# Last block of a fused attention and bilinear feed-forward kernel: which accumulators share a PSUM tile, and when its side work is issued

## The chip, the cores and the metric

The kernel runs on one core of one Trainium2 chip. Its time is the device time of one execution in microseconds (us). A core has five engines, each with its own queue, which it works through in order: PE (TensorE, matrix products, with the weight loads PEld), DVE (VectorE), ACT (ScalarE), POOL (GpSimd) and SP (SyncE, which here issues DMAs). They wait for one another by semaphores.

## The reference

One layer on x of shape 1 x 2048 x 576: multi-query attention with 32 heads of width 18 that share one key and one value, then a gated feed-forward part of width F = 4608 without a nonlinearity.

```python
h  = x + attention(layernorm(x)) @ wo
z  = layernorm(h)
g  = z @ w_gate            # 2048 x 4608
u  = z @ w_up              # 2048 x 4608
h2 = h + (g * u) @ w_down  # 2048 x 576
```

Everything is float32. The kernel reaches that accuracy by splitting each operand into a high part (a cast) and a low part (the rest, a subtraction on DVE) and by making three products of each: high by high, high by low, low by high.

## The kernel before, in words

The 2048 rows are four blocks b = 0 to 3 of 512 rows (TB). Blocks 0 to 2 go through `ffn(b)` (L905), while the attention of the later blocks runs in between. `ffn` loops over 36 feature tiles f of 128 columns. For each f, 27 pairs of matmuls (L930, numbered j) make g and u; then ACT copies g (L956), DVE multiplies it by u (L960, `hf`), and after every second f the products are added to the output by `down` (L843) for a pair of feature tiles. `down` makes 14 stages of three matmuls (L882) in three accumulators; each stage is read and added to the residual h, by DVE (L888) or by an ACT copy and a POOL addition (L892, L893), and a stage that goes on in the same accumulator waits for that reading. The last pair of a block has a simpler form (L855): eight outputs, one after another.

While there is attention left, g and u have a tile of one bank each; once it is used up (block 2, f from 23 on), they share a tile of two banks (L922).

PSUM has eight banks. `ps_s` (L69) gives tiles of two banks, two of them; `ps_f` one bank, two of them; `ps_m` and `ps_a` one bank, one of each.

Two pieces of side work are generators that `ffn` steps at fixed j:

- `weight_sums` (L1076): sums of gate and up weights that the last block needs. POOL makes 72 of them (L1087), with loads and stores by SP; the loop takes one step at j = 8, 16 and 24 of each f of blocks 0 and 1 (L939). Its two buffers are taken from the ten in which the weights of `down` are held.
- `ahead` (L982): what the last block needs before it begins. Four steps normalise its h (DVE L990, POOL L991); five transpose it, 4 PE transposes (L998) and an ACT copy (L999) each; the others make sums and high and low parts on ACT and DVE (L1016 to L1032), and the first weight parts. When they are taken is set by two tables by hand: AHEAD (f: {j: steps}) and TURNS (steps after the `down` at the end of f), L1470 on.

The last block (`last_block`, L1119) computes g and u by a seven-product scheme over halves of 256 rows (Strassen's idea). It loops over 18 passes p. Each pass has seven `product` calls of 12 matmuls (L1138), three `tail` calls of 4 (L1145), and between them up to seven steps of `down` for earlier passes (`go`, generator D). The accumulators are `a` (of this pass, changing place from pass to pass), `b_` and `c`. In the order of the program:

- product 1 into a, ACT copy (L1176), a step of down;
- product 2 and tail into c, DVE sum (L1182), POOL product, step;
- product 3 into b_, ACT copy (L1188), step; product 4 into a, ACT copy (L1195), step;
- product 5 and tail into b_, DVE sum (L1201); product 6 and tail into a, DVE sum (L1207), two steps;
- product 7 and tail into a, a step, ACT copy of one half (L1237), DVE product of the other half with it (L1240).

Between these stand the high parts (ACT, L1154) and low parts (DVE, L1157) for the later down. After each product `feed(i)` (L1052) is called: DVE makes the low part of the gate and up weights for the product two further on (L1058), ACT the high part for the one three further on (L1061), and SP loads a later one. So the low weights of product 2 of a pass are made by the last instruction that DVE has in the pass before.

`down_pairs` (L1092) does down for two passes at once: seven steps, each for t = 0 and 1 (two row halves), into four accumulators, two for each t; each result is read by DVE (L1108), or for four of the 14 by ACT (L1112) and POOL (L1113). At the end the last pair of feature tiles is added by eight outputs (L1262) with a DVE addition each (L1266) and four stores.

In the kernel before, `a` takes turns between the two halves of the `ps_s` tile s0, and b_ and c are the halves of s1; down_pairs has ps_f, ps_f, ps_m and ps_a.

## Time and profile before

| | |
|---|---|
| median of 3 runs | 2356.39 us (2353.79 to 2359.95) |
| profiled execution, its time | 2357.88 us |
| its span, first to last instruction | 2356.1 us |
| mean granted TensorE clock in it | 0.995 |
| busy: PE, ACT, DVE, POOL | 96%, 64%, 54%, 30% |

The last block's passes begin at about 1965 us of the span. Rows of a timeline show the start (us from the span's start), the duration (us), engine, line, operation, output<-inputs, the count of merged instructions and, in brackets, the idle time before and what ended it. Rows of windows show a stretch, its length and the busy time of PE, PEld, DVE, ACT and POOL with the instructions in it, then the granted TensorE clock, the DMA share and GB/s. Rows of waits show microseconds in total, how often, and the longest.

### The profile page before, as it was taken

How to read it: one execution, taken by the hardware profiler on the slowest of the kernel's cores; microseconds unless marked ns; L12 is line 12 of the kernel's file. 1: busy time of each engine (PE TensorE's matmuls, PEld its weight loads, DVE VectorE, ACT ScalarE, POOL GpSimd, SP SyncE). 2: the span in 40 equal slices, each digit the busy share in tenths (PEclk: the TensorE clock that was granted, in tenths of full speed). 3: DMA queues.
4: the chain of work that ended last, by engine and by line, in shares of the span. 5: the costliest groups of instructions: out<-in, count | busy, mean ns of one | idle time of the engine just before them, and what ended most of it. 6: DMA issues, size and time to landing. Idle time of an engine off the chain costs nothing.

```text
span 2356.1 us, 46348 instructions
## 1 busy us (share of the span) xinstructions
PE 2270.4 (96%) x17958; PEld 1644.1 (70%) x17958; DVE 1269.4 (54%) x2209; ACT 1509.7 (64%) x2046; POOL 714.0 (30%) x826
## 2 busy tenths in 40 slices
PE   7999999999999999999999999999999999888888
PEld 5333345777777777777777777677777878888888
DVE  7565644444444455445454555444444766667665
ACT  6888877767676766677767666676767234444443
POOL 5345301333333333233333333221222332122222
PEclk9999999999999999999999999999999999999999
DMA  5778834555455556555555445533333545656664
GB/s 176 241 257 302 278 135 132 163 161 165 155 167 163 163 164 204 168 166 172 166 167 170 155 149 181 173 120 107 120 118 114 171 150 163 196 195 203 205 207 148
DMA packets 199126, 407.05 MB, mean 173 GB/s; under 512 B 21325, under 2 KB 52941, under 8 KB 198901
## 3 DMA queue, kind: packets, MB, share of 16 engines
q1 hardware_dynamic: 196165, 392.78, 51.5%
q0 software_dynamic: 2736, 11.26, 1.5%
q8 instruction: 143, 2.34, 0.4%
q14 instruction: 82, 0.67, 0.1%
HBM read 317.27 MB, written 74.55 MB: 166 GB/s over the span
## 4 chain that ended last, share of the span: by engine, by line
PE 77%; DVE 7%; DMA 1%; ACT 1%; issue 1%; SPq 0%; POOL 0%; DVEq 0%; ACTq 0%
PE pg L930 21%; PE acc L611 15%; PE y L882 13%; PE s L606 9%; PE gs L1138 7%; PE pu L930 3%; PE yq L1104 3%; PE yo L736 3%; PE gu L930 2%; PE gs L1145 1%; DVE XW L1157 1%; DVE wt L1074 1%; DVE wrs L1058 1%; ACT P L607 0%; DMA raw<-wsum_dram 0%
## 5 line engine op out<-in xcount | busy, mean ns | idle before, releaser
L607 ACT ACTIVATE P<-s 128x1024 f32<-128x1024 f32 x1024 | 1026.4, 1027 | 286.1 <-PE s L606 204.4
L930 PE MATMUL pu<-X,ws 64*128 64x512 f32 x2565 | 694.1, 389 | 0.1
L930 PE MATMUL pg<-X,ws 64*128 64x512 f32 x2565 | 693.3, 389 | 0.1
L930 PEld LDWEIGHTS pg<-X,ws 64*128 64x128 f32 x2565 | 475.3, 185 | 70.3 <-DMA wsum<-in_wgs_dram 0.8
L611 PE MATMUL acc<-P,V 128*32 128x512 f32 x4096 | 492.1, 600 | 0.7 <-ACT P L607 0.6
L930 PEld LDWEIGHTS pu<-X,ws 64*128 64x128 f32 x2565 | 472.9, 185 | 6.9 <-DMA X<-X 0.4
L606 PE MATMUL s<-q,kT 56*128 56x512 f32 x2048 | 440.6, 423 | 6.0 <-ACT P L607 3.1
L893 POOL TENSOR_TENSOR h<-h,tmp 128x288 f32<-128x288 f32 x306 | 238.6, 809 | 603.2 <-ACT tmp L892 602.0
L606 PEld LDWEIGHTS s<-q,kT 56*128 56x128 f32 x2048 | 198.7, 184 | 206.0 <-ACT P L607 120.6
L882 PEld LDWEIGHTS y<-wdo,room 128*128 128x128 f32 x2142 | 291.1, 189 | 46.4 <-issue 34.8
L882 PE MATMUL y<-wdo,room 128*128 128x288 f32 x2142 | 304.6, 301 | 5.0 <-DVE h L888 5.0
L611 PEld LDWEIGHTS acc<-P,V 128*32 128x32 f32 x4096 | 114.5, 109 | 247.2 <-issue 240.9
L888 DVE TENSOR_TENSOR h<-h,y 128x288 f32<-128x288 f32 x408 | 176.5, 452 | 198.8 <-PE y L882 198.7
L892 ACT COPY tmp<-y 128x288 f32<-128x288 f32 x306 | 122.3, 400 | 241.7 <-PE y L882 225.0
L960 DVE TENSOR_TENSOR hf<-pu,g 128x512 f32<-128x512 f32 x95 | 65.7, 692 | 303.2 <-ACT g L956 303.1
L92 POOL CAST ws<-wr 128x1152 fp32r<-128x1152 f32 x108 | 127.3, 1179 | 301.7 <-PE pu L930 224.7
L93 DVE TENSOR_TENSOR ws<-wr,ws 128x1152 fp32r<-128x1152 f32 x108 | 176.7, 1636 | 61.1 <-POOL ws L92 60.8
L1087 POOL TENSOR_TENSOR wsum<-wsum,wsum 128x512 f32<-128x512 f32 x72 | 98.1, 1363 | 174.1 <-DMA wsum<-in_wgs_dram 174.1
L93 DVE TENSOR_TENSOR room<-S,room 128x1024 fp32r<-128x1024 f32 x51 | 62.8, 1231 | 135.3 <-ACT room L92 135.3
L1138 PE MATMUL gs<-XS,wrs 128*128 128x256 f32 x432 | 63.5, 299 | 40.7 <-DVE hfl L1240 40.7
L1138 PEld LDWEIGHTS gs<-XS,wrs 128*128 128x128 f32 x432 | 58.2, 202 | 45.4 <-DVE hfl L1240 45.0
L1104 PE MATMUL yq<-wdo,XW 128*128 128x288 f32 x504 | 87.4, 302 | 1.0 <-DVE h L1108 0.9
(245 smaller groups left out, 2669.2 us busy)
## 6 DMA issues: line engine op xcount, KB each, us to landing
wdo<-wd_dram SPq DMA_DIRECT2D x492, 288.0 KB
wr<-in_wgu_dram SPq DMA_DIRECT2D x108, 576.0 KB
wsum<-in_wgs_dram SPq DMA_DIRECT2D x108, 256.0 KB
wd_dram<-wd_room SPq DMA_DIRECT2D x20, 1008.0 KB
wsum_dram<-wsum SPq DMA_DIRECT2D x72, 256.0 KB
raw<-wsum_dram SPq DMA_DIRECT2D x72, 256.0 KB
q<-q_dram SPq DMA_DIRECT2D x64, 216.0 KB
raw<-in_wgs_dram SPq DMA_DIRECT2D x54, 256.0 KB
```

Source lines behind the costliest of these rows:

```text
L92: (copy or self.cast)(hi, src)
L93: self.dve.tensor_tensor(lo, src, f32(hi), ALU.subtract)
L606: self.pe.matmul(s_[:, i], self.kT[o:o + 56, t * P:(t + 1) * P], q[o:o + 56, pr], start=True, stop=True)
L607: self.act.activation(p_, s_, AF.Exp, scale=SCALE)
L611: self.pe.matmul(acc[32 * j:32 * j + 32, :], self.V[:, t, :], Ps[j // 2][:, j % 2, :], start=(t == 0), stop=(t == NT - 1), skip_group_chec ...
L882: pe.matmul(y[:, :HD], m[:, t * P:(t + 1) * P], k, start=(first and j == 0), stop=(j == 2), skip_group_check=True)
L888: dve.tensor_tensor(hs, hs, y[:, :HD], ALU.add)
L892: act.copy(z, y[:, :HD])
L893: pool.tensor_tensor(hs, hs, z, ALU.add)
L930: pe.matmul(ps, w[o:o + 64, wk, c], X[o:o + 64, xk, c], start=(j == 0), stop=(j == 26))
L1104: pe.matmul(y[:, :HD], A[:, k, x, t * P:(t + 1) * P], v[:, l], start=(first and z == j == 0), stop=(z == len(pairs) - 1 and j == 2), skip_ ...
L1138: pe.matmul(bank[:, g * HT:(g + 1) * HT], W[:, wk, c, g], X[:, 2 * xk + c], start=(first and g == c == wk == xk == 0), stop=(c == 1 and wk ...
```

## The change

- In the last block, `a` takes turns between two `ps_f` tiles (one bank each), b_ is the `ps_m` tile and c the `ps_a` tile. `down_pairs` takes two `ps_s` tiles, one for each t, of which the two halves are its two accumulators. The last eight outputs and the down of block 2's last pair are placed accordingly; the latter two also use halves of `ps_s` tiles.
- The normalisation of the last block's h is taken at f = 29 instead of 28, all five transpose steps after the down of f = 30 instead of two after 28 and three after 30, with four accumulators instead of two; of the other steps, eight instead of six are at f = 31 and four instead of six at f = 33.
- `weight_sums` takes no step at the first and last f of a block; the steps that are left run in the first feature tiles of block 2, and its two buffers come free there.

```diff
@@ down, last pair of a block
             for s in range(NQ):
+                if b == NB - 2:
+                    e = self.ps_s(f"y{b}_{pair}_{s}")
                 for n in range(2):
-                    ys[s, n] = self.ps_y(2 * s + n, f"y{b}_{pair}_{s}_{n}")
+                    ys[s, n] = e[:, n] if b == NB - 2 else self.ps_y(2 * s + n, f"y{b}_{pair}_{s}_{n}")
@@ ffn
-                    if b < 2 and j in (8, 16, 24):
-                        next(self.sums, None)
+                    if 0 < f < NF - 1 and j in (8, 16, 24) and self.sums:
+                        if next(self.sums, "end") == "end":
+                            self.sums = None
+                            self.load_wd(self.n_wd + 2)
...
-        self.load_wd(self.n_wd + (6 if b == 1 else 4))
+        self.load_wd(self.n_wd + 4)
@@ ahead
-            ps = (self.ps_m if c % 2 else self.ps_a)(f"txl{c}")
+            ps = (self.ps_a, self.ps_m, self.ps_f, self.ps_f)[c % 4](f"txl{c}")
@@ down_pairs
-        banks = [self.ps_f(f"yq{pairs[0]}_0"), self.ps_f(f"yq{pairs[0]}_1"), self.ps_m(f"yq{pairs[0]}_2"), self.ps_a(f"yq{pairs[0]}_3")]
+        banks = [self.ps_s(f"yq{pairs[0]}_{t}") for t in range(2)]
...
-                y = banks[2 * bank + t]
+                y = banks[t][:, bank]
@@ last_block
-        s0, s1 = self.ps_s("gs0"), self.ps_s("gs1")
+        gs = [self.ps_f("gs0"), self.ps_f("gs1")]
+        b_, c = self.ps_m("gs2"), self.ps_a("gs3")
...
-            a, b_, c = s0[:, p % 2], s1[:, 0], s1[:, 1]
+            a = gs[p % 2]
...
-                y = (s0, s1)[k // 2][:, k % 2] if k < 4 else self.ps_y(k - 4, f"ye{k}")
+                if k in (4, 6):
+                    e = self.ps_s(f"ye{k}")
+                y = (gs[0], b_, c, gs[1])[k] if k < 4 else e[:, k % 2]
@@ tables
-AHEAD = {28: {6: 1, 9: 1, 12: 1, 15: 1}, 31: {3: 1, 7: 1, 11: 1, 15: 1, 19: 1, 23: 1}, 32: {6: 1, 13: 1}, 33: {4: 1, 8: 1, 12: 1, 16: 1, 20: 1, 24: 1},
-         34: {10: 1}, 35: {5: 1, 11: 1, 17: 1, 23: 1}}
-TURNS = {28: 2, 30: 3}
+AHEAD = {29: {5: 1, 10: 1, 15: 1, 20: 1}, 31: {2: 1, 5: 1, 8: 1, 11: 1, 14: 1, 17: 1, 20: 1, 23: 1}, 32: {6: 1, 13: 1},
+         33: {4: 1, 9: 1, 14: 1, 19: 1}, 34: {10: 1}, 35: {5: 1, 11: 1, 17: 1, 23: 1}}
+TURNS = {30: 5}
```

## The prediction

> **What bounds the kernel now.** I read the page first, then the waits of PE, then the timeline where PE waits.

> ```profile
> span 2356.1 us, 46348 instructions
> PE 2270.4 (96%) x17958; PEld 1644.1 (70%) x17958; DVE 1269.4 (54%) x2209; ACT 1509.7 (64%) x2046; POOL 714.0 (30%) x826
> PE 77%; DVE 7%; DMA 1%; ACT 1%; issue 1%; SPq 0%; POOL 0%; DVEq 0%; ACTq 0%
> ```

> PE is busy for 96% of the span, and the chain that ended last is PE for 77%. So only time in which PE stands still, or runs slowly, can be won. Windows say where that is:

> ```profile
> 920.00:1472.00 552.00, 550.65 (x4534) 405.39 (x4534) 277.65 (x452) 376.37 (x485) 183.65 (x189) 1.00 0.53 170
> 2007.00:2343.00 336.00, 298.73 (x2297) 290.36 (x2297) 225.52 (x432) 148.72 (x317) 74.84 (x83) 0.98 0.60 195
> ```

> The first busy column is PE. Block 1 has 1.4 us idle in 552, so nothing is to be had inside it. The last block has 37 us idle in 336. The waits of PE name the cause:

> ```profile
> PE gs L1138 <- DVE hfl L1240: 40.7, 17, 2.9
> ...
> PE gs L1262 <- DVE h L1266: 1.2, 2, 0.6
> ```

> Seventeen times, once between any two of the 18 passes, product 1 waits for L1240. That DVE instruction reads `a` of the pass before, in the other half of the same `ps_s` tile; product 1 uses nothing that it writes. The second row is the same thing at the end: an output waits for the addition that reads the other half of its tile. So waits are ordered by the tile, not by the bank.

> **The change in a pass.** Single-bank tiles take the wait for L1240 away. What is late next? Two passes in the timeline (passes 9 and 10, the tail of 8 ahead of them):

> ```profile
> 2148.42 0.69 DVE L1207 TENSOR_TENSOR gu<-gs,cs 128x512 f32<-128x512 f32 x1 [0.54 <-PE gs L1145]
> ...
> 2154.88 1.70 PE L1138 MATMUL gs<-XS,wrs 128*128 128x256 f32 x12 [2.15 <-DVE hfl L1240]
> ...
> 2156.10 0.68 DVE L1058 TENSOR_TENSOR wrs<-raw,wrs 128x512 fp32r<-128x512 f32 x1
> ...
> 2156.42 0.99 PE L1104 MATMUL yq<-wdo,XW 128*128 128x288 f32 x6
> ...
> 2157.24 1.60 PE L1138 MATMUL gs<-XS,wrs 128*128 128x256 f32 x12
> ...
> 2160.18 1.49 PEld L1138 LDWEIGHTS gs<-XS,room 128*128 128x128 f32 x12 [0.29 <-DVE gu L1182]
> ...
> 2168.71 0.69 DVE L1207 TENSOR_TENSOR gu<-gs,cs 128x512 f32<-128x512 f32 x1 [0.54 <-PE gs L1145]
> ...
> 2175.64 1.70 PE L1138 MATMUL gs<-XS,wrs 128*128 128x256 f32 x12 [2.63 <-DVE hfl L1240]
> ...
> 2176.86 0.69 DVE L1058 TENSOR_TENSOR wrs<-raw,wrs 128x512 fp32r<-128x512 f32 x1
> ...
> 2195.89 1.70 PE L1138 MATMUL gs<-XS,wrs 128*128 128x256 f32 x12 [2.16 <-DVE hfl L1240]
> ```

> The L1058 that starts at 2176.86 makes the low weights of product 2, whose third matmul needs them. It ends at 2177.55. PE was free at 2175.64 - 2.63 = 2173.01; with 1.6 for product 1, 1.0 for a step of down, each overlapping the next a little, and two matmuls it would stand at that third matmul at about 2175.8. So PE waits there instead, for some 1.8 us. The gain is not the 2.6 us that the row shows, but what lies between the two waits.

> That is a loop, and its length is the new pass. From the start of L1207 DVE has work without a long pause to the end of this L1058 (windows of the clock part that lie in such runs show it busy for 3.30 us of 3.40): 2177.55 - 2168.71 = 8.84 us in an odd pass, 2156.78 - 2148.42 = 8.36 in an even one. Its order is unchanged. From the end of L1058 to the next L1207, PE sets the pace: from the start of product 2 it takes 2168.71 - 2157.24 = 11.47 us now. In it product 3 waits 0.29 for L1182, which reads the other half of `s1`; with tiles of their own that goes, so 11.19. Before, product 2 began 0.46 after the L1058; now its first two matmuls are done by then and ten are left, as if it had begun 0.1 before it. So 11.09, and the passes become 8.36 + 11.09 = 19.45 (even; now 2195.89 - 2175.64 = 20.25) and 19.93 (odd; now 2175.64 - 2154.88 = 20.76). Eight even passes save 0.80, seven odd ones (3 to 15) 0.83: **12.2 us** for passes 2 to 16. The last pass keeps the part before its L1207: **0.8**.

> Pass 1 has almost no steps of down and is a loop already:

> ```profile
> 1987.92 0.68 DVE L1058 TENSOR_TENSOR wrs<-raw,wrs 128x512 fp32r<-128x512 f32 x1
> ...
> 1992.00 1.70 PE L1138 MATMUL gs<-XS,room 128*128 128x256 f32 x12 [0.85 <-DVE gu L1182]
> ...
> 1995.74 1.45 PE L1138 MATMUL gs<-XS,wps 128*128 128x256 f32 x10 [0.36 <-DVE wps L1058]
> ...
> 1999.58 0.69 DVE L1207 TENSOR_TENSOR gu<-gs,cs 128x512 f32<-128x512 f32 x1 [0.54 <-PE gs L1145]
> ```

> The third row is the wait that I expect everywhere, ten matmuls of a product held by L1058, 1.45 us long. Here the 0.85 for L1182 goes, and the same 0.56 ahead of product 2 as in the other passes (0.46 and 0.1): **1.4**.

> `down_pairs` now has two accumulators in a tile, so a step for t waits for the reading of the step before it for the same t. Inside the passes another step and at least one product of 1.6 us lie between, and the readings stand early enough in DVE's and ACT's queues: nothing. After the last pass nothing lies between:

> ```profile
> 2338.97 1.65 DVE L1108 TENSOR_TENSOR h<-h,yq 128x288 f32<-128x288 f32 x4
> 2339.47 4.74 PE L1104 MATMUL yq<-wdo,XW 128*128 128x288 f32 x30 [0.89 <-DVE h L1108]
> ```

> PE now has four steps done when DVE comes to the first addition; then it would have two. Two steps of 0.45 and a turn of about 0.5 for each of the others cost about 1.0. The last eight outputs lose the two waits of 0.6 and get two others like them, at the fifth and the seventh pair; a copy more or less on ACT is hidden. I take **-0.6** for the end (bounds +0.6 and -1.5).

> **The change in the feed-forward tiles.**

> ```profile
> 1890.62 1.35 DVE L93 TENSOR_TENSOR ws<-wr,ws 128x1152 fp32r<-128x1152 f32 x1
> ...
> 1891.89 2.04 DVE L990 TENSOR_SCALAR xhl<-h,mvb,yb 128x576 f32<-128x576 f32 x4
> ...
> 1893.85 0.81 DVE L888 TENSOR_TENSOR h<-h,y 128x288 f32<-128x288 f32 x2
> ...
> 1894.35 6.09 PE L882 MATMUL y<-wdo,room 128*128 128x288 f32 x33 [3.19 <-DVE h L888]
> ...
> 1928.82 0.69 DVE L960 TENSOR_TENSOR hf<-gu,g 128x512 f32<-128x512 f32 x1 [0.18 <-ACT g L956]
> ...
> 1936.33 4.70 PE L882 MATMUL y<-wdo,room 128*128 128x288 f32 x33 [0.73 <-DVE h L888]
> ```

> At f = 28 the four normalisations stand in DVE's queue ahead of the additions of down, and PE waits 3.19. At f = 29 no down follows, and DVE has room. The additions then start at 1891.9: the wait shrinks by **1.95**, not to nothing, since the weight split ahead of them still ends at 1891.97. It then also no longer halves the clock (below), **1.6**.

> At f = 31 there are now eight steps: two more low parts on DVE of 0.6 each, ahead of a product that had only 0.18 to spare, and the five transposes in a row delay its start by 0.2. So the additions after f = 32, which come late already (0.73), come about 1.2 later: **-1.2** (bounds 0 and -2.9, that with a halved stretch of clock).

> ```profile
> 1470.44 1.27 POOL L1087 TENSOR_TENSOR wsum<-wsum,wsum 128x512 f32<-128x512 f32 x1
> ...
> 1472.35 0.76 DVE L93 TENSOR_TENSOR wos<-wor,wos 128x576 fp32r<-128x576 f32 x1 [2.24 <-POOL wos L92]
> ...
> 1474.42 0.53 PE L855 MATMUL y<-wdo,room 128*128 128x288 f32 x2 [1.29 <-ACT room L92]
> ```

> At the end of block 1 a sum stands ahead of a cast on POOL, DVE waits 2.24 for that cast, then `hf` is late, and PE waits 1.3. Without the sum the cast comes 1.2 earlier: **1.2**. Four sums and their loads move to block 2, where POOL has more room and blocks 0 and 1 show them at no cost to PE; eight weight buffers instead of ten for four tiles served blocks 0 and 1 as well: nothing (bounds 0 and -2).

> **The clock.** PE's clock is halved for stretches of 3.4 us:

> ```profile
> 1894.10:1897.50 3.40, 3.15 (x13) 3.15 (x14) 1.02 (x3) 0.80 (x2) 1.60 (x3) 0.50 0.59 203
> 2006.80:2010.20 3.40, 3.40 (x18) 3.40 (x17) 1.65 (x3) 1.16 (x3) 0.00 (x0) 0.50 0.23 81
> ...
> 2047.70:2051.10 3.40, 1.56 (x13) 1.57 (x14) 3.30 (x9) 2.23 (x5) 0.00 (x0) 1.00 0.64 215
> ...
> 2088.70:2092.10 3.40, 1.53 (x12) 1.53 (x13) 3.30 (x9) 2.23 (x5) 0.00 (x0) 1.00 0.64 213
> 2092.10:2095.50 3.40, 3.40 (x18) 3.40 (x17) 1.43 (x3) 1.10 (x2) 0.00 (x0) 0.50 0.22 77
> ...
> 2112.60:2116.00 3.40, 3.40 (x17) 3.40 (x17) 1.62 (x4) 1.85 (x5) 0.00 (x0) 0.50 0.17 56
> ```

> The column behind POOL's is the clock. A window with 1.53 us of PE work was followed by a halved one, one with 1.56 was not; so a wait counts if some 1.85 us of it fall into one window. In the last block that happened four times (from 2006.8 to 2112.6, one of them not shown), for at most 1.7 us each, half of 3.4. The waits to come are about 1.6 us in an even pass, too short, and 2.1 in an odd one. Passes of 19.4 and 19.9 do not stay in step with the windows as now, and about half of the eight odd ones should hit: four as before, **0** (bounds +6 and -7).

> [...]

> **Sum.** 12.2 + 0.8 + 1.4 - 0.6 + 1.95 + 1.6 - 1.2 + 1.2 = 17.3 us off the profiled execution's 2357.88 (its span and 1.8 around it): 2340.6. The median is 1.5 below that execution: **2339.0 us**.

> **Rivals.**

> - *Full removal.* If DVE kept ahead, all of PE's 40.7 and the 17 waits of 0.29 would go: 45.6 instead of 14.4 in the passes, some 2308. Against it: DVE has no gap between L1207 and L1058, and its work there is not changed. 0.05.
> [...]
> - *Each odd wait halves the clock.* Four more: 2345. 0.08.
> - *The tiles are not the cause,* product 1 waits as before and only the feed-forward part gains: 2353. Against it, no other operand of product 1 comes from L1240. 0.05.
> - *Slower.* Two accumulators in a tile make each step of down wait for the last reading. A turn is 0.6 (the waits of L1262); with 14 steps in each of nine calls, if all of it were bare, 76 us on top of 2339, so 2415. It decides when a step starts less than 0.6 after the end of the last one for the same t, or when the additions stand behind the 8 us run on DVE by a step. Products lie between everywhere but at the end. 0.04.

> **How the numbers follow.** The forecast has the rest, 0.66. Errors of 0.3 in the length of a pass are 5 us, and the clock moves it by 6: 2329 to 2348 holds it, both cases of the clock, and leaves out full removal and the last two. A measurement of this kernel tells about 0.3% (7 us) from no change. Faster: forecast, full removal and both cases of the clock, 0.91; within 0.3%: 0.05; slower: 0.04.

> **What would show it.** PE's wait for L1240 is gone from the waits; in its place product 2 waits for `wrs` L1058, in a row of ten matmuls, 17 times by some 1.6 to 2.1 us. L1207 to the end of that L1058 still takes 8.4 and 8.8. Passes start 19.4 and 19.9 apart. The wait after f = 28 is near 1.2 and that after f = 32 near 1.9. If product 1 still waits for DVE, or no product waits for L1058, the loop is wrong.

## The result, and the profile after

The changed kernel takes 2347.76 us (median of 7 runs, 2346.70 to 2351.78). The kernel before took 2356.39 on the same chip (7 runs, 2353.79 to 2359.95). The ratio is 0.9966, with a 95% interval of 0.9954 to 0.9977: faster by 8.6 us. The direction is the predicted one and the time lies in the range, but half of the predicted gain of 17.3 is missing. The profiled execution took 2346.70, its span 2344.9 at a mean clock of 0.993.

The page, and two windows, those of block 1 and of the last block:

```profile
span 2344.9 us, 46338 instructions
PE 2270.2 (97%) x17958; PEld 1649.9 (70%) x17958; DVE 1272.4 (54%) x2209; ACT 1506.7 (64%) x2046; POOL 714.5 (30%) x826
PE 76%; DVE 7%; ACT 1%; DMA 1%; issue 1%; SPq 0%; DVEq 0%; ACTq 0%
```

```profile
920.00:1472.00 552.00, 551.02 (x4538) 402.28 (x4537) 281.35 (x458) 377.64 (x487) 180.05 (x186) 1.00 0.53 168
2007.00:2343.00 336.00, 303.19 (x2312) 297.61 (x2311) 226.85 (x437) 145.61 (x314) 73.74 (x82) 0.96 0.62 196
```

In the last block PE's idle time fell from 37 to 33 us, but the granted clock (the number behind POOL's) fell too, from 0.98 to 0.96. That second number is the story of this case.

The waits of PE:

```profile
PE gs L1143 <- DVE wrs L1062: 31.8, 17, 2.4
PE y L884 <- DVE h L890: 5.3, 4, 3.0
PE yq L1108 <- DVE h L1112: 1.6, 3, 1.3
...
PE ye L1269 <- DVE h L1273: 1.1, 2, 0.5
```

(L1143 is L1138 of before, L1062 is L1058, L1212 is L1207, L1245 is L1240, L1036 is L1032, L884 and L890 are L882 and L888; in down_pairs PE's L1108 and DVE's L1112 are L1104 and L1108. The experiments' numbers are up to three off these.) The wait of product 1 for L1245 is gone from the list. In its place stands a wait for the weights, 17 times. The row of yq and that of ye are waits at the end, for tiles that two accumulators share. In the timeline, around passes 9 and 10 and again near the end:

```profile
2145.18 1.46 PE L1143 MATMUL gs<-XS,wrs 128*128 128x256 f32 x10 [1.66 <-DVE wrs L1062]
...
2156.20 0.69 DVE L1212 TENSOR_TENSOR gu<-gs,cs 128x512 f32<-128x512 f32 x1 [0.54 <-PE gs L1150]
...
2164.37 0.69 DVE L1062 TENSOR_TENSOR wrs<-raw,wrs 128x512 fp32r<-128x512 f32 x1
2165.11 1.46 PE L1143 MATMUL gs<-XS,wrs 128*128 128x256 f32 x10 [2.13 <-DVE wrs L1062]
...
2168.67 2.13 PE L1143 MATMUL gs<-XS,room 128*128 128x256 f32 x12
...
2186.09 1.46 PE L1143 MATMUL gs<-XS,wrs 128*128 128x256 f32 x10 [1.65 <-DVE wrs L1062]
...
2267.80 1.46 PE L1143 MATMUL gs<-XS,wrs 128*128 128x256 f32 x10 [1.66 <-DVE wrs L1062]
...
2287.69 1.46 PE L1143 MATMUL gs<-XS,wrs 128*128 128x256 f32 x10 [2.12 <-DVE wrs L1062]
```

It is the row of ten matmuls that was forecast. From the start of L1212 to the end of the L1062 in question it is 2165.06 - 2156.20 = 8.86 us (forecast 8.84). From 2267.80 to 2287.69 is an undisturbed pass of 19.89 (forecast 19.93). But from 2145.18 to 2165.11 to 2186.09 it is 19.93 and then 20.98, and the row between shows why: the twelve matmuls of product 3 take 2.13 there instead of 1.6. PE's clock is halved. Windows show where such stretches come from:

```profile
2162.95:2166.35 3.40, 1.27 (x11) 1.24 (x11) 2.97 (x7) 2.33 (x5) 0.00 (x0) 1.00 0.40 147
2166.50:2169.90 3.40, 3.40 (x17) 3.40 (x16) 1.29 (x2) 0.92 (x2) 1.53 (x2) 0.50 0.59 173
2203.95:2207.35 3.40, 1.33 (x11) 1.33 (x12) 2.88 (x7) 2.33 (x5) 0.00 (x0) 1.00 0.38 135
2207.50:2210.90 3.40, 3.40 (x17) 3.40 (x17) 1.29 (x2) 0.92 (x2) 1.67 (x2) 0.51 0.66 187
2244.90:2248.30 3.40, 1.43 (x12) 1.43 (x13) 2.82 (x6) 2.33 (x5) 0.00 (x0) 1.00 0.35 122
2248.40:2251.80 3.40, 3.40 (x18) 3.40 (x17) 1.29 (x2) 0.92 (x2) 1.81 (x2) 0.50 0.66 200
...
2285.85:2289.25 3.40, 1.56 (x13) 1.56 (x14) 2.68 (x6) 2.24 (x5) 0.00 (x0) 1.00 0.36 129
2289.35:2292.75 3.40, 3.40 (x30) 3.40 (x29) 1.36 (x3) 1.72 (x5) 1.81 (x2) 1.00 0.77 232
```

Read them in pairs: a window in which PE works 1.27, 1.33 or 1.43 us is followed by one at clock 0.50; the one with 1.56 is not. The pairs stand 41.0 us apart, and they began at 2002.7: seven halved stretches in the passes (2002.7, 2043.6, 2084.6, 2125.6, 2166.5, 2207.5, 2248.4), where the prediction had four as before. One more is at 2326.9, after the last pass.

By stages, from the starts of the same instructions in the two timelines: until block 0's end (its code unchanged but for the sums) -1.2 us and block 1 -1.7 (forecast nothing for either), block 2 with the end of block 1 -1.6 (forecast -3.55), the passes up to the last L1207/L1212 -10.1 (forecast -14.4), from there on +3.4 (forecast +0.6). The sum is -11.2, the difference of the two spans; the runs' medians differ by 8.6, since the profiled execution of the changed kernel was its fastest (1.1 under its median) and that of the kernel before lay 1.5 above its own.

### The profile page after: what moved, and what is told of

Read it like the earlier page. It is cut to its first block, busy times and chain, and to the rows that moved or that the text cites. A ratio compares the mean times of both kernels' runs of the same rounds, so it can differ in the third digit from the quotient of the medians.

```text
span 2344.9 us, 46338 instructions
## 1 busy us (share of the span) xinstructions
PE 2270.2 (97%) x17958; PEld 1649.9 (70%) x17958; DVE 1272.4 (54%) x2209; ACT 1506.7 (64%) x2046; POOL 714.5 (30%) x826
## 4 chain that ended last, share of the span: by engine, by line
PE 76%; DVE 7%; ACT 1%; DMA 1%; issue 1%; SPq 0%; DVEq 0%; ACTq 0%
PE pg L932 21%; PE acc L611 15%; PE y L884 13%; PE s L606 9%; PE gs L1143 5%; PE pu L932 4%; PE yq L1108 3%; PE yo L736 2%; PE gu L932 2%; PE gs L1150 1%; DVE wrs L1062 1%; DVE XW L1162 1%; PE y L855 1%; DVE wt L1078 1%; DVE h L1112 0%
## 5 line engine op out<-in xcount | busy, mean ns | idle before, releaser
L895 POOL TENSOR_TENSOR h<-h,tmp 128x288 f32<-128x288 f32 x306 | 238.4, 807 | 613.2 <-ACT tmp L894 612.0
L884 PEld LDWEIGHTS y<-wdo,room 128*128 128x128 f32 x2142 | 291.3, 189 | 47.1 <-issue 34.8
L884 PE MATMUL y<-wdo,room 128*128 128x288 f32 x2142 | 304.9, 301 | 5.4 <-DVE h L890 5.3
L890 DVE TENSOR_TENSOR h<-h,y 128x288 f32<-128x288 f32 x408 | 175.6, 452 | 200.8 <-PE y L884 200.6
L92 POOL CAST ws<-wr 128x1152 fp32r<-128x1152 f32 x108 | 126.6, 1173 | 326.5 <-PE pu L932 242.6
L93 DVE TENSOR_TENSOR ws<-wr,ws 128x1152 fp32r<-128x1152 f32 x108 | 181.5, 1680 | 60.8 <-POOL ws L92 59.5
L93 DVE TENSOR_TENSOR room<-S,room 128x1024 fp32r<-128x1024 f32 x51 | 62.5, 1226 | 133.5 <-ACT room L92 133.5
L1143 PE MATMUL gs<-XS,wrs 128*128 128x256 f32 x432 | 62.6, 287 | 31.8 <-DVE wrs L1062 31.8
L1108 PE MATMUL yq<-wdo,XW 128*128 128x288 f32 x504 | 91.7, 311 | 1.6 <-DVE h L1112 1.6
L1153 POOL TENSOR_TENSOR hfl<-gu 128x256 f32<-128x256 f32 x36 | 33.1, 919 | 170.4 <-DVE gu L1187 156.5
```

The lines of the kernel that those rows point to most:

```text
L92: (copy or self.cast)(hi, src)
L93: self.dve.tensor_tensor(lo, src, f32(hi), ALU.subtract)
L884: pe.matmul(y[:, :HD], m[:, t * P:(t + 1) * P], k, start=(first and j == 0), stop=(j == 2), skip_group_check=True)
L890: dve.tensor_tensor(hs, hs, y[:, :HD], ALU.add)
L895: pool.tensor_tensor(hs, hs, z, ALU.add)
L1108: pe.matmul(y[:, :HD], A[:, k, x, t * P:(t + 1) * P], v[:, l], start=(first and z == j == 0), stop=(z == len(pairs) - 1 and j == 2), skip_ ...
```

## The experiments

Nine kernels, each timed in five rounds against the kernel before on the same chip (before: 2357.14, 2356.03 and 2355.79 us in the three sets). Halved stretches were counted in windows of 0.4 us, in one execution of each kernel. The changed kernel wasn't timed again in these sets: "less than the changed kernel" is the difference from its 2347.76, and the medians of before differ between sets by up to 1.4.

### What sets a pass: the place of the low parts in DVE's queue

If the run of DVE from L1212 to this L1062 is the loop, then the L1062 for product 2 only has to be issued earlier. Two edits of the changed kernel:

```diff
# e1_feed_small
                 low(1, a12)
+                self.feed(i + 6)
                 low(6, S[:, 3])
-            self.feed(i + 6)
+            if end:
+                self.feed(i + 6)
# e2_feed_early
             tail(1, 2, a)
+            self.feed(i + 6)
...
-            self.feed(i + 6)
```

> The changed kernel, with the weight part of the last feed of a pass (L1062 in it) put ahead of the last low part instead of behind it, so some 0.37 us earlier in DVE's order. Loop theory: the wait of product 2 for L1062 falls by 0.37 in each of 17 passes, to about 1.3 and 1.75 us: 6 us, 2341.5. Clock theory on top of it (a wait that fills 1.85 of a 3.4 us window halves the clock for the next one, at 1.5 us each): no wait is long enough any more, the seven halved stretches in the passes go, another 10 us: 2331. If the halved stretches cost nothing because PE waits for DVE anyway, 2341.5.

> The changed kernel, with that feed put right behind product 7 and its tail, ahead of all low parts of the end of the pass (some 4.5 us earlier in DVE's order). Loop theory: the loop through L1062 is broken; the next one late is the weight part for product 3, behind the whole run on DVE, by about 0.3 us in odd passes. Passes of about 17.9 and 18.2 instead of 19.4 and 19.9 (27 us), and no halved clock (10 us): about 2310. Rival: DVE is at its limit in this stretch and the low parts that come later hold down back, so that the wait comes back there: 2335 to 2345.

e1 took 2333.26 us (2328.63 to 2341.30; ratio 0.9902 [0.9880, 0.9925]), e2 2308.88 (2305.62 to 2310.56; ratio 0.9795 [0.9773, 0.9816]). PE's waits in e2, and two of its rows a pass apart:

```profile
PE gs L1143 <- DVE room L1062: 3.2, 8, 0.7
```

```profile
2140.77 1.60 PE L1143 MATMUL gs<-XS,wrs 128*128 128x256 f32 x12
...
2158.95 1.60 PE L1143 MATMUL gs<-XS,wrs 128*128 128x256 f32 x12
```

The 31.8 us of waiting are gone but for 3.2, now at product 3, and this pass is 18.18 long. So the place of that one subtraction in DVE's queue, at the end of the run that starts with L1212, was the loop. (The edit moves the whole feed, ACT's high part and a load with it; but it is L1062 that the waits name.) Moving it past a single instruction (e1) takes 7.4 us off the waits (31.8 to 24.4), but the time falls by 14.5. The rest is mostly clock: e1 has three halved stretches in the passes (2001.8, 2080.3 and 2158.8) instead of seven, and four fewer at 1.55 are 6.2. I expected none; its odd waits are about 1.72, and its runs spread over 12.7 us.

### Is it the clock? PE kept busy while it waits

A direct test leaves the loop as it is and only fills the wait of product 2. Matmuls whose result nobody uses (c is started afresh by product 2) stand ahead of it:

```diff
+            for _ in range(4 if p else 0):      # e8_fill_four; 8 in e9_fill_eight
+                pe.matmul(c[:, 0:HT], self.WS[(i + 1) % 7][:, 0, 0:P], self.XS[NAMES[1]][:, 0],
+                          start=True, stop=True, skip_group_check=True)
             product(i + 1, c, True)
```

> The changed kernel with four more matmuls of 128x256 ahead of product 2 of passes 2 to 18; they write c, which product 2 starts afresh, so nothing uses their result. PE does them in time in which it waits for L1062 now: 4 x 0.14 = 0.6 us, and the wait falls from 1.66 and 2.12 to about 1.1 and 1.55. Clock theory (a window of 3.41 us with too little work of PE halves the next, and seven stretches of the passes are halved for that, each costing 1.55 us): most or all of the seven go, the passes keep 19.4 and 19.9, and the time is 2347.8 - 10.9 = 2337 or a little above. Rival (the waits aren't what halves the clock, or a halved stretch is hidden): the stretches stay, 2347.8, or longer by 17 x 0.6 = 10, 2358, if PE and not DVE's run of work set the pass.

> The same with eight such matmuls, 1.15 us in each of 17 passes: the wait falls to about 0.5 and 1.0. Clock theory: no halved stretch between 2000 and 2320 us, the passes keep 19.4 and 19.9, about 2337, though PE does 20 us more of work. Rival (stretches come of something else): 2347.8; or, if PE set the pass, 2367.

e8 took 2337.45 us (2336.65 to 2337.76; ratio 0.9921 [0.9907, 0.9934]), e9 2334.48 (2333.14 to 2337.77; ratio 0.9913 [0.9899, 0.9927]). So 68 and 136 useless matmuls made the kernel 10.3 and 13.3 us faster. The waits of e9, two of its passes, and its windows (the last block's, and two where the changed kernel is halved):

```profile
PE gs L1143 <- DVE wrs L1062: 15.6, 17, 1.4
```

```profile
2138.53 1.46 PE L1143 MATMUL gs<-XS,wrs 128*128 128x256 f32 x10 [0.70 <-DVE wrs L1062]
2158.47 1.46 PE L1143 MATMUL gs<-XS,wrs 128*128 128x256 f32 x10 [1.18 <-DVE wrs L1062]
2177.88 1.46 PE L1143 MATMUL gs<-XS,wrs 128*128 128x256 f32 x10 [0.70 <-DVE wrs L1062]
```

```profile
2007.00:2333.00 326.00, 305.10 (x2417) 299.25 (x2415) 225.84 (x435) 144.82 (x311) 73.91 (x82) 1.00 0.63 201
2002.50:2005.90 3.40, 3.40 (x29) 3.40 (x29) 1.29 (x2) 1.43 (x4) 1.82 (x2) 1.00 0.74 227
...
2166.50:2169.90 3.40, 3.40 (x30) 3.40 (x29) 1.97 (x4) 0.67 (x2) 1.12 (x1) 1.00 0.86 264
```

The passes are 19.94 and 19.41, the same as the undisturbed ones of the changed kernel, so DVE's run still sets them; the clock is 1.00 throughout, and no stretch between 2000 and 2330 is halved. e8 keeps two (2002.4 and 2316.4). In the passes, up to the last L1212 (L1214 here), the three profiled executions can be compared directly: 357.0 us with seven halved stretches (changed kernel), 347.8 with one (e8), 346.1 with none (e9), so about 1.55 for each.

### The two parts of the change

e4 is the kernel before with the PSUM tiles of the last block alone; e5 is the changed kernel with the PSUM tiles of before, so that only the moves in the feed-forward part are left.

```diff
# e4_banks_only: before, with (here in part)
-        s0, s1 = self.ps_s("gs0"), self.ps_s("gs1")
+        gs = [self.ps_f("gs0"), self.ps_f("gs1")]
+        b_, c = self.ps_m("gs2"), self.ps_a("gs3")
...
-                y = banks[2 * bank + t]
+                y = banks[t][:, bank]
# e5_rest_only: the same lines turned back in the changed kernel
```

> The kernel before with the last block's PSUM tiles of the changed one alone (f = 28, the transposes and the sums as before). Loop and clock theory: passes save 14.4 us by the loop, pay 4.5 for three more halved stretches, and the end loses 3: about 7 us under the kernel before, 2349. If the shortfall came from the feed-forward part instead, 2342.

> The changed kernel with the last block's PSUM tiles of the kernel before; normalisation, transposes, AHEAD and the sums as changed. By the traces: 1.2 to 1.7 at the end of block 1, 1.1 in the first tiles of block 2, 3.5 at f = 28, lost again at f = 32 (2.3 of wait and 1.6 of halved clock): about 3 us under the kernel before, 2353. If the parts depend on each other through the phase of the clock's windows, up to 6 us on either side.

e4 took 2351.66 us (2347.33 to 2356.12; ratio 0.9977 [0.9964, 0.9989]), e5 2353.17 (2351.50 to 2358.24; ratio 0.9988 [0.9976, 0.9999]). Against 2357.14 that is -5.5 and -4.0, together -9.5, where the whole change gives -8.6: the parts add up. The waits of e5, then of e4:

```profile
PE gs L1140 <- DVE hfl L1242: 40.8, 17, 2.9
```

```profile
PE gs L1141 <- DVE wrs L1060: 31.8, 17, 2.4
```

The tiles alone decide which of the two waits there is. e4 has the halved stretches of the passes again 41 us apart, from 2005.4 to 2292.1, eight of them; e5, with the old waits, has two (1983.5 and 2003.9). So the new tiles bring the row of halved stretches with them, eight in e4 against the four of the kernel before, and that takes back part of what they gain.

### The wait after f = 32

```diff
# e3_ahead_six: the changed kernel with the steps of f = 31 and 33 of before
-31: {2: 1, 5: 1, 8: 1, 11: 1, 14: 1, 17: 1, 20: 1, 23: 1}
+31: {3: 1, 7: 1, 11: 1, 15: 1, 19: 1, 23: 1}
-33: {4: 1, 9: 1, 14: 1, 19: 1}
+33: {4: 1, 8: 1, 12: 1, 16: 1, 20: 1, 24: 1}
```

> The changed kernel with six steps at f = 31 and six at f = 33 as before, the rest as changed. If the two more steps at f = 31 are what holds DVE up, the wait after f = 32 falls from 3.0 to about 0.9 us and the halved stretch behind it goes: 3.5 us, about 2344. If the five transposes in a row are the cause, the wait stays near 3 and the time at 2348.

e3 took 2343.45 us (2342.66 to 2347.80; ratio 0.9947 [0.9931, 0.9963]), 4.3 less than the changed kernel. In the changed kernel the timeline after f = 28 and after f = 32 shows (with it DVE's work ahead of the second wait):

```profile
1887.55 4.70 PE L884 MATMUL y<-wdo,room 128*128 128x288 f32 x33 [1.23 <-DVE h L890]
...
1919.45 2.23 DVE L1036 TENSOR_TENSOR XS<-xtl,XS 128x512 fp32r<-128x512 f32 x2
...
1926.74 1.35 DVE L93 TENSOR_TENSOR ws<-wr,ws 128x1152 fp32r<-128x1152 f32 x1
...
1928.01 1.28 DVE L1036 TENSOR_TENSOR XS<-xsums,XS 128x512 fp32r<-128x512 f32 x1
1929.21 0.68 DVE L1036 TENSOR_TENSOR XS<-xtl,XS 128x512 fp32r<-128x512 f32 x1
1929.81 0.81 DVE L890 TENSOR_TENSOR h<-h,y 128x288 f32<-128x288 f32 x2
1930.31 6.18 PE L884 MATMUL y<-wdo,room 128*128 128x288 f32 x33 [3.04 <-DVE h L890]
```

and the waits of e3:

```profile
PE y L884 <- DVE h L890: 3.1, 4, 1.2
```

In e3 the longest of these waits is 1.2 instead of 3.04 (that after f = 32 is 0.86), and the halved stretch at 1931 is gone, so the 33 matmuls behind the wait no longer take 6.18 instead of 4.70. The two steps that came to f = 31 are its cause. Two low parts (L1036) stand right ahead of the additions of down in e3 too, 0.68 each. What e3 lacks is two of the three low parts that the changed kernel has ahead of the product `hf` at 1922.2 (the first two took 2.23 together); and none of its low parts here takes 1.28.

### The end

```diff
# e6_end_apart: the changed kernel; the last down gets four tiles of one bank, the last eight outputs the others
-        banks = [self.ps_s(f"yq{pairs[0]}_{t}") for t in range(2)]
+        if apart:
+            one = [self.ps_f("yl0"), self.ps_m("yl1"), self.ps_a("yl2"), self.ps_f("yl3")]
+        else:
+            banks = [self.ps_s(f"yq{pairs[0]}_{t}") for t in range(2)]
...
-                y = banks[t][:, bank]
+                y = one[2 * bank + t] if apart else banks[t][:, bank]
```

> The changed kernel, in which the last call of down (that for one pair, behind the last pass) has four tiles of one bank, as before the change, and the last eight outputs have the two-bank tiles first. If the shared tile is what made the end 3.4 us longer, 1.3 to 3 us come back (the second if the halved stretch there goes too): 2345 to 2346.5. If DVE's additions bound the end by themselves, nothing: 2348.

e6 took 2344.43 us (2343.09 to 2346.39; ratio 0.9945 [0.9930, 0.9961]), 3.3 less. The end of the changed kernel, then of e6:

```profile
2324.95 1.05 PE L1108 MATMUL yq<-wdo,XW 128*128 128x288 f32 x6 [1.26 <-DVE h L1112]
...
2326.16 6.88 PE L1108 MATMUL yq<-wdo,XW 128*128 128x288 f32 x30 [0.15 <-DVE h L1112]
```

```profile
2325.26 2.10 PE L1111 MATMUL yl<-wdo,XW 128*128 128x288 f32 x12
...
2327.96 4.73 PE L1111 MATMUL yl<-wdo,XW 128*128 128x288 f32 x30 [0.61 <-DVE h L1115]
```

Thirty matmuls take 6.88 us at the end of the changed kernel and 4.73 in e6. Two things are in that. With two accumulators in a tile PE waits for each addition; and the clock is halved there too (0.50), from 2326.9 on. The traces of e3 and e9 tell them apart: they have the shared tile, but no halved stretch in this place, and there (in e3) the same thirty take

```profile
2323.03 6.01 PE L1108 MATMUL yq<-wdo,XW 128*128 128x288 f32 x30 [0.15 <-DVE h L1112]
```

From the last L1212 to the end of the span it is 23.4 us in the kernel before, 25.9 in e3 and e9, 26.8 in the changed kernel and 23.5 in e6: 2.5 for the sharing, 0.9 for the clock. In e3 the steps of three matmuls start 0.5 to 0.7 us apart there, in the kernel before 0.4.

### All of it together

e7_all has the edits of e2, e3 and e6.

> The early feed, the six steps and the end with tiles of its own together. Sum of their expectations: 27 + 10 + 3.5 + 1.3 to 3 under the changed kernel, about 2305. If they share gains (the halved stretches counted twice), 2309.

It took 2300.89 us (2299.70 to 2301.45; ratio 0.9760 [0.9743, 0.9777]), the fastest of all and better than both kernels, by 55 and 47 us. Its mean clock is 0.999. The runs of the changed kernel spread over 5.1 us and those of e1 over 12.7; e7's spread over 1.8, and its profiled execution has no halved stretch in the last block. That this is why the spread is small fits, but wasn't tested.

## What the prediction had right, and which step failed

The loop was right; the number of halved stretches, a term set to 0, was wrong, and two smaller terms (f = 31 and the end) were too small. Against the forecast of 17.35 us the two profiled executions lack 4.3 in the passes, 2.8 at the end and 1.95 in block 2, and have 2.9 in blocks 0 and 1 that weren't forecast: 11.2 in all. Part of those 2.9 was chance.

- **The bound and the cause** (a wait ordered by the tile, not the bank): right. e4 and e5 show the wait for L1240 coming and going with the tiles alone.
- **The next wait and its size**: right. L1062, product 2, ten matmuls, 17 times, 1.66 and 2.12 (forecast "some 1.6 to 2.1"); undisturbed passes 19.42 and 19.89 (forecast 19.45 and 19.93). e2 shows that it is the loop. The term of 12.2 + 0.8 + 1.4 is what the passes win when the clock is left out: those of e9, without a halved stretch, are 20.9 us shorter than before, of which the four stretches of before at 1.55 are 6.2, and 14.7 are left.
- **"The clock. ... four as before, 0"**: this step failed. The price per stretch (at most 1.7) was right, their number was not: seven instead of four (eight in e3, e4 and e6, which have the same waits). Three more at 1.55 (20.98 less 19.42) are 4.7 us; 14.4 - 10.1 = 4.3 are missing in the passes. e8 and e9 show that the clock is the cause: with PE busy in the same waits, the stretches go and so does the time. My reasoning took the odd waits as independent of one another, of which about half would fall badly. They aren't. Two passes are 39.3 us, and 40.9 when one is halved. The halved stretches (hits) stand (2248.4 - 2002.7) / 6 = 40.95 us apart. In the clock records of the trace each of them lasts 3.41 us, and 40.95 is 12 times that; the four in the passes of the kernel before start at 2006.77, 2027.25, 2092.11 and 2112.59, so 6, 19 and 6 times 3.41 apart. So in both executions they keep to one beat of 3.41 us; what sets it, no run shows. My estimate from these distances: a hit brings the next odd wait to nearly the same place of the beat, and the row of hits holds itself up until it has drifted out: PE's work in the thin window rises from 1.27 to 1.33, 1.43 and 1.56. That the stretches stand 41 us apart in the changed kernel, e3, e4 and e6 agrees with this. So does e1, which has another length of pass: two passes are 38.5 us, and 40.0 with a halved stretch, which is no whole multiple of 3.41 (11.7), but four passes with one such stretch are 78.5, 23 times 3.41, and its three hits stand 78.5 apart. Why a row begins and where it ends is argued, not shown: no kernel shifts the beat and leaves the waits as they are.
- **f = 31, -1.2** (bounds 0 and -2.9): a mis-sized term. The wait after f = 32 is 3.04 where 1.9 was forecast, with a halved stretch behind it: (3.04 - 0.73) + (6.18 - 4.70) = 3.8 us. I had counted two more low parts at 0.6 each; ahead of `hf` two took 2.23 together, and one behind it 1.28 instead of 0.68. e3 takes it back: 4.3.
- **The end, -0.6** (bounds +0.6 and -1.5): a mis-sized term, outside its bounds: +3.4 us in time instead of +0.6. The wait for a shared tile was foreseen, but at about 1.0; the sharing alone costs 2.5 (e3 and e9), since PE waits for every addition of the last call. The halved stretch at 2326.9, which wasn't foreseen, adds 0.9. e6 wins 3.3 by taking the sharing away.
- **f = 28 and the end of block 1**: right. The wait after f = 28 is 1.23 (forecast 1.24) and its halved stretch is gone; at the end of block 1 PE waits 0.19 instead of 1.29:

```profile
1468.35 0.76 DVE L93 TENSOR_TENSOR wos<-wor,wos 128x576 fp32r<-128x576 f32 x1 [1.02 <-POOL wos L92]
...
1470.42 0.53 PE L855 MATMUL y<-wdo,room 128*128 128x288 f32 x2 [0.19 <-ACT room L92]
```

- **The sums, "blocks 0 and 1 show them at no cost to PE"**: a term put at nothing that wasn't. In block 2, where four sums went, no wait on PE names them: right. But taking the sums out of the feature tiles on both sides of the end of block 0 won 1.2 of block 1's 1.7. In the kernel before, SP issues two loads of sums there ahead of eight copies within X (L797), and the last copy is issued 1.8 us later against PE's work than in the changed kernel. In the first tile of block 1 PE's weight loads wait for these copies, which they don't in the changed kernel. Rows of before:

```profile
936.28 0.18 PEld L930 LDWEIGHTS pg<-X,ws 64*128 64x128 f32 x1 [0.41 <-DMA X<-X]
...
936.90 0.18 PEld L930 LDWEIGHTS pu<-X,ws 64*128 64x128 f32 x1 [0.44 <-DMA X<-X]
```

  From the first matmul of L930 in that tile to the last it is 8.55 us in before and 8.31 in e4, which keep these sums, and 7.35 to 7.37 in the nine kernels without them. That the order of SP's queue is the reason is read from the traces; no run changes it alone.
- **Chance**: the 1.2 us until block 0's end are there at the first matmul of its `ffn` already (377.6 us instead of 378.8), ahead of every changed line. The kernel before had a halved stretch at 54.4 us in this execution, the changed one none there; e6, with the same code up to there and a halved stretch at 54.8, is at 379.2.

## What to carry to other kernels

When a wait is taken out of a loop, price the one that takes its place and then ask how much work PE has in each 3.4 us around it: of two waits of 2.13 and 2.12 us in the changed kernel (those that end at 2165.11 and 2287.69) the first had a halved stretch behind it, which cost some 1.55 us, and the second had none; in this loop seven such stretches came in a row, 40.95 us apart. If a wait can't be removed, matmuls that nobody needs may pay for themselves (68 of them took 10.3 us off in e8); better is to look for what is last in another engine's queue and issue it earlier, which here was worth 39 us for one moved line. Put accumulators that are read and refilled in turn into tiles of their own: sharing made 40.7 us of waits in the passes of the kernel before, and cost 2.5 us at the end of the changed one.

## What the runs showed of the hardware

```profile
2076.85:2080.25 3.40, 1.68 (x14) 1.47 (x14) 3.22 (x8) 2.33 (x5) 0.00 (x0) 1.00 0.48 174
2080.35:2083.75 3.40, 3.40 (x18) 3.40 (x17) 1.29 (x2) 0.92 (x2) 1.61 (x2) 0.51 0.57 177
...
2323.40:2326.80 3.40, 1.98 (x13) 1.48 (x12) 1.94 (x5) 0.70 (x2) 0.79 (x1) 1.00 0.74 243
```

- More work on PE shortened the time in e9: 136 useless matmuls, which fill 16.2 us of the waits (31.8 to 15.6), took 13.3 us off.
- The longer runs of the changed kernel had the lower clock: they took 2346.70 us at a mean clock of 0.993, 2349.70 at 0.991 and 2351.78 at 0.989.
- Some subtractions on DVE took longer beside a product or an addition on POOL. In the changed kernel 19 of the 36 L1062 that write `wrs` (128x512) had none beside them and took 0.68 to 0.69 us, 17 had one and took 0.86 to 1.22. The L1036 of 1.28 had one beside it as well (L895). But the L1062 that write `wps` and `wss` took 0.68 to 0.69 both with POOL's L1153 beside them (36) and without (36), so POOL alone doesn't explain it.
